# Rows of x first on ScalarE, an exponential ahead of copies, constants loaded later

## The chip, the core and the metric

The kernel runs on one core of a Trainium2 chip. Five engines work side by side, each on its own queue in program order: TensorE (PE) multiplies, VectorE (DVE), ScalarE (ACT) and GpSimd (POOL) work on elements, SyncE (SP) issues loads. 16 transfer engines move data. TensorE writes to PSUM, in eight banks, from which VectorE or ScalarE copy into SBUF. The metric is the time of one execution on the device in microseconds. Before the change three runs gave 613.08, 617.48 and 619.69, median 617.48.

## What is computed

Attention of 8 batches and 8 heads on 576 positions with 64 dimensions: the first four heads look at the last 32 positions, the other four at every 32nd one. Its result, as 4608 rows x of 512, goes through a mixture of 8 experts: each row to the one expert of the largest gate logit.

```python
scores = np.where(masks[None, :, :, :], scale * np.matmul(q, k.transpose(0, 1, 3, 2)), -1000000000.0)
attn = np.exp(scores - np.max(scores, axis=-1, keepdims=True))
attn = attn / (np.sum(attn, axis=-1, keepdims=True) + 1e-09)
x = np.matmul(attn, v)            # then as rows: [4608, 512]
logits = x @ w_gate               # [4608, 8]
expert_idx = np.argmax(logits, axis=1)
for e in range(E):
    mask = expert_idx == e
    h = np.maximum(x[mask] @ w1[e], 0.0)
    out[mask] = gate_w[mask, None] * (h @ w2[e])
```

## The kernel before

**Attention.** Each batch has five tasks (`BANK_PAIRS`), each one PSUM bank of scores: tasks 0 and 1 the local heads, 2 to 4 the rest and the strided heads. A task is worked in a pipeline over the loop index `i` (the loop at lines 977 to 1023, where the order of TensorE is as written):
- `stage_s`: a matmul that writes the mask into the bank (line 480), score matmuls on it (491 for tasks 0 and 1, 499 and 505 for the others), then `softmax`: largest value (407) and subtraction (411) on VectorE, the exponential (412) on ScalarE, sum (414) and reciprocal (416) on VectorE, the product with the reciprocal (421) on GpSimd.
- `stage_t`, three tasks later: four transposes of the probabilities on TensorE (542), copied from PSUM by ScalarE (`evac`, line 169), into `pTl` with two copies for tasks 0 and 1, into `pT` with one for the others.
- `av_local`, `av_strided`, four tasks later: the products with v (567, 556), copied by ScalarE into `xT`.

Tasks 3 and 4 are scored together, so four sets of scores of batch 0 come ahead of the first copies. `load_qk` and `load_v` issue the loads of q, k and v on SyncE's queue up to five tasks ahead, when the buffer is free; those of the first batch come one behind the other.

**Rows and routing.** Two batches make a group of 1152 rows. `logits` multiplies `xT` with the gate weights (616), and finds the gate; `xrows` transposes 128 rows back on TensorE (608), copies them from PSUM on ScalarE into `xr`, behind which GpSimd has written the gate in 16 columns (605), and stores them from ScalarE's queue (611). There are 36 such row tiles. They and the logits share two banks of PSUM (`XTAGS`: y for the first two groups, v for the others), so a copy that is late holds up whatever takes the bank next. `route` computes each row's place in its expert's list (matmuls 675, 677, 658), `slot_tables` the tables for the rows beyond the base lists.

**Experts.** From about 118 us on, the expert windows on the first three groups (`fillers`) run between the attention tasks; after the attention come the rest of them, then the base windows of all experts. Weights are loaded in 1 MB pieces (228), split into two parts by ScalarE (238) and VectorE (239), and used by three matmuls each (331 to 333, 320 to 322).

**Start.** ScalarE's queue first issues three loads: mask and identity (960), gate weights `wg` (390), and `cst` (391), the constants of the routing: a triangle, the numbers 0 to 127 and others. `load_more` also converts them: the triangle on VectorE (393), the numbers on GpSimd (398, 399).

**Order.** On engines other than TensorE a scheduler sets the order, by a priority that falls with the place in the program; `tc.high_priority(offset=n)` lifts instructions by n places. `issue_after(a, b)` puts a behind b on their queue without a wait.

Of the kernel before, what the change touches and what calls it, by code (L numbers as in the profile page):

```python
# [13 lines left out]
ALU = mybir.AluOpType  # L14
# [6 lines left out]
E, DM, DF = 8, 512, 1024  # L21
# [9 lines left out]
GT = GB * S // 128  # L31
# [27 lines left out]
X_ENG = "aa"  # L59
# [91 lines left out]
def moe_attn(ctx, tc, qk, vv, wg, wcat, blob0, blob, out):  # L151
    nc = tc.nc
# [10 lines left out]
    def evac(which, out, in_):  # L163
        if which == "v":
            nc.vector.tensor_copy(out=out, in_=in_)
        elif which == "g":
            nc.gpsimd.tensor_copy(out=out, in_=in_)
        else:
            copied[0] = nc.scalar.copy(out=out, in_=in_)

    copied = [None]
# [5 lines left out]
    cst = const.tile([128, blob.shape[1]], F32, name="cst")  # L177
    tri_f = cst[:, 0:128]
    iota_sb = cst[:, 128:256]
    wexp_sb = cst[:, 256:256 + E]  # L180
    tokhi_sb = cst[:, 256 + E:256 + E + NT]
# [51 lines left out]
    after = []  # L233
# [35 lines left out]
    def issue_after(ins, prev):  # L269
        tc.add_manual_dep(ins.ins, prev.ins.name,  # L270
                          mybir.DependencyInfo(mybir.DependencyClass.NoSync, mybir.DependencyReason.SCHED_ONLY),
                          reason="order on the engine's queue")
# [84 lines left out]
    with ExitStack() as actx:  # L357
# [29 lines left out]
                                      in_=lmask_f[:, 64 * m:64 * m + 64].unsqueeze(1).broadcast_to([128, x1 - x0, 64]))  # L387

        def load_more():
            nc.scalar.dma_start(out=wg_sb.rearrange("p c e -> p (c e)"), in_=wg)  # L390
            nc.scalar.dma_start(out=cst, in_=blob)
            nc.vector.memset(ones_b, 1.0)
            nc.vector.tensor_copy(out=tri_b, in_=tri_f)
            for t in (pfall, tokp, keyp, keysp):
                nc.gpsimd.memset(t, 0.0)
            for t in ex_tiles:
                nc.gpsimd.memset(t[:, :, E:], EPS)
            nc.gpsimd.tensor_copy(out=tokp[:, :, 0:GT], in_=tokhi_sb.rearrange("p (g t) -> p g t", t=GT))
            nc.gpsimd.tensor_copy(out=iota2, in_=iota_sb.unsqueeze(2).broadcast_to([128, 128, 2]))
            zrow = xrp.tile([128, XW], F32, name="xr")[0:1]  # L400
            nc.gpsimd.memset(zrow, 0.0)
            nc.gpsimd.dma_start(out=xd[0:1, :], in_=zrow)

        def softmax(sb):
            sv = sb.rearrange("p (n k) -> p n k", k=64)[:, :, 0:USED]
            nm = small.tile([128, 8], F32, name="nm")
            largest = nc.vector.tensor_reduce(out=nm, in_=sv, axis=AX.X, op=ALU.max)
            prob = next_prob()
            whole = prob.rearrange("p (n k) -> p n k", k=64)
            pv = whole[:, :, 0:USED]  # L410
            shifted = nc.vector.tensor_tensor(out=pv, in0=sv, in1=nm.unsqueeze(2).broadcast_to([128, 8, USED]), op=ALU.subtract)
            exps.append(nc.scalar.activation(out=pv, in_=pv, func=AF.Exp, scale=0.125))
            sm = small.tile([128, 8], F32, name="sm")
            total = nc.vector.tensor_reduce(out=sm, in_=whole, axis=AX.X, op=ALU.add)
            ri = small.tile([128, 8], F32, name="ri")
            begun.append((largest, shifted, total, nc.vector.reciprocal(out=ri, in_=sm)))  # L416
            if len(begun) == 3:
                issue_after(begun[1][0], begun[0][2])
                issue_after(begun[2][0], begun[0][3])
                issue_after(begun[1][2], begun[2][1])  # L420
            product[0] = nc.gpsimd.tensor_tensor(out=pv, in0=pv, in1=ri.unsqueeze(2).broadcast_to([128, 8, USED]), op=ALU.mult)  # L421
            return prob

        loaded = {}
        exps = []
        begun = []

        def in_order(d, b):
            if b == 0:
# [20 lines left out]
        def load_qk(i):  # L450
            if i < len(tasks):
                b, k = tasks[i]
                x = halves(qk, b, QKO, k)
                if k < 2:
                    for h in range(2):
                        in_order(nc.sync.dma_start(out=two(qkl[k][h:128:2, h * LK:h * LK + LQ + LK]),
                                                   in_=x[h:128:2]), b)
                    return
                t = inp.tile([128, max(QKW[2:])], F32, name="qk")
                loaded[b, "qk", k] = t  # L460
                in_order(nc.sync.dma_start(out=two(t[:, 0:QKW[k]]), in_=x), b)
# [68 lines left out]
        def stage_s(b, *ks):  # L530
            sb = [bank("s") for _ in ks]
            gens = [scores(b, k, s) for k, s in zip(ks, sb)]
            for _ in zip_longest(*gens):
                pass
            return [softmax(s) for s in sb]
# [3 lines left out]
        def stage_t(b, k, prob):  # L539
            tb = bank("t")  # L540
            for x in range(4):
                nc.tensor.transpose(tb[:, x * 128:(x + 1) * 128], prob[:, x * 128:(x + 1) * 128], ident)
            if k < 2:
                evac("a", pTl[k][0:64, 0, :], tb[0:64, :])
                evac("a", pTl[k][64:128, 1, :], tb[64:128, :])
                return
            pT = pts.tile([128, 512], F32, name="pT")
            evac("a", pT, tb)
            pTs[b, k] = pT
# [53 lines left out]
        def xrows(g, c, xT):  # L603
            xr = xrp.tile([128, XW], F32, name="xr")
            nc.gpsimd.tensor_copy(out=xr[:, DM:XW], in_=gates[g][:, c:c + 1].broadcast_to([128, XW - DM]))
            xb = bank(XTAGS[g])
            for pr in range(4):
                nc.tensor.transpose(xb[:, pr * 128:(pr + 1) * 128], xT[:, pr, c * 128:(c + 1) * 128], ident)
            evac(X_ENG[c % 2], xr[:, 0:DM], xb)
            T = g * GT + c  # L610
            nc.scalar.dma_start(out=xd[1 + T * 128:1 + (T + 1) * 128, :], in_=xr)

# [165 lines left out]
        def slot_tables():  # L778
# [1 line left out]
            nc.vector.scalar_tensor_tensor(out=rem, in0=tiles_sb, scalar=-128.0, in1=cnt, op0=ALU.mult, op1=ALU.add)  # L780
            nc.vector.tensor_scalar(out=rem, in0=rem, scalar1=0.0, scalar2=None, op0=ALU.max)
            it128 = rt.tile([128, 32], F32, name="it128")
            nc.vector.tensor_scalar(out=it128, in0=iota_sb[:, 0:32], scalar1=128.0, scalar2=None, op0=ALU.mult)
            cmp = scratch(E * 32).rearrange("p (e k) -> p e k", k=32)
            nc.vector.tensor_tensor(out=cmp, in0=rem.unsqueeze(2).broadcast_to([128, E, 32]),
                                    in1=it128.unsqueeze(1).broadcast_to([128, E, 32]), op=ALU.is_gt)
# [189 lines left out]
        with tc.manual_schedule(engines={mybir.EngineType.PE}):  # L976
            for i in range(nt + LAG_AV):
                it = i - LAG_T
                if 0 <= it < nt:
                    stage_t(*tasks[it], pvs.pop(it))  # L980
                step()
                ia = i - LAG_AV
                if 0 <= ia < nt:
                    b, k = tasks[ia]
                    g, bb = divmod(b, GB)
                    if g not in xTs:
                        xTs[g] = xtp.tile([128, 4, GB * S], F32, name="xT")
                        Ls[g] = rt.tile([128, GT, E], F32, name="L", bufs=2)
                        dls[g] = rt.tile([128, GT, E], F32, name="dl", bufs=2)
                        gates[g] = rt.tile([128, GT], F32, name="gt", bufs=2)  # L990
                    step()
                exps.clear()
                if i < nt:
                    filling()
                    b, k = tasks[i]
                    if k == PAIR[0]:
                        pvs[i], pvs[i + 1] = stage_s(b, *PAIR)
                    elif k not in PAIR:
                        pvs[i], = stage_s(b, k)
                    load_qk(i + NBK)  # L1000
                if 0 <= ia < nt:
                    b, k = tasks[ia]
                    if k == 0:
                        queue.extend(late)
                        late.clear()
                    elif k == 1:
                        av_local(b, xTs[g], bb * S)
                    elif k == 3:
                        av_strided(b, 0, xTs[g], bb * S)
                        for e in exps:  # L1010
                            issue_after(e, copied[0])
                    elif k == 4:
                        av_strided(b, 1, xTs[g], bb * S)
                        for e in exps:
                            issue_after(e, copied[0])
                        (late if b < EG * GB - 1 else queue).extend(row_steps(g, bb, xTs[g], Ls[g]))
                        if b == B - 1:
                            filling()
                if 0 <= ia:
                    load_v(ia + NV - 1)  # L1020
                step()
                filling()
                step()
# [348 lines left out]
```

## Time and profile before

| | |
|---|---|
| median of three runs | 617.48 us |
| the profiled execution | 617.55 us |
| its span | 615.8 us |
| TensorE busy | 588.2 us, 96% |
| VectorE, ScalarE, GpSimd busy | 349.9, 284.2, 153.9 us |
| moved by the transfer engines | 133.04 MB, 216 GB/s in the mean |

TensorE is the busiest engine by far. Its idle time lies in the first 215 us and at the very end; a stretch of the profile tells which engine it waited for there. The granted clock is the one at which TensorE's array runs, 1.00 for 2.4 GHz and 0.50 for 1.2 GHz. An idle time stands in brackets at the instruction that ended it, with what released it.

### The profile page before, as it was taken

How to read it: one execution, taken by the hardware profiler on the slowest of the kernel's cores; microseconds unless marked ns; L12 is line 12 of the kernel's file. 1: busy time of each engine (PE TensorE's matmuls, PEld its weight loads, DVE VectorE, ACT ScalarE, POOL GpSimd, SP SyncE). 2: the span in 40 equal slices, each digit the busy share in tenths (PEclk: the TensorE clock that was granted, in tenths of full speed). 3: DMA queues.
4: the chain of work that ended last, by engine and by line, in shares of the span. 5: the costliest groups of instructions: out<-in, count | busy, mean ns of one | idle time of the engine just before them, and what ended most of it. 6: DMA issues, size and time to landing. Idle time of an engine off the chain costs nothing. (4 is left out here: it accounts for less than half of the span.)

```text
span 615.8 us, 14290 instructions
## 1 busy us (share of the span) xinstructions
PE 588.2 (96%) x5930; PEld 489.5 (80%) x5930; DVE 349.9 (57%) x684; ACT 284.2 (46%) x508; POOL 153.9 (25%) x202
## 2 busy tenths in 40 slices
PE   5899989989899999999999999999999999999996
PEld 3677766768788788888888998788988879987885
DVE  6779878868653699975534445234443335452342
ACT  2566757755755555645333434324333324442241
POOL 4333332431220331060630332014402003020031
PEclk9899999999999999999999999999999999999999
DMA  8989989997557666595862565355644537254101
GB/s 293 306 290 337 333 265 341 364 357 257 184 177 286 211 235 226 184 347 195 297 230 81 191 208 177 122 212 195 217 171 172 205 132 288 79 177 147 60 38 53
DMA packets 43203, 133.04 MB, mean 216 GB/s; under 512 B 4602, under 2 KB 17280, under 8 KB 34944
## 3 DMA queue, kind: packets, MB, share of 16 engines
q1 hardware_dynamic: 29504, 89.14, 42.3%
q10 hardware_dynamic: 7344, 22.71, 10.1%
q0 software_dynamic: 6288, 20.26, 9.0%
q8 instruction: 47, 0.77, 0.5%
q14 instruction: 20, 0.16, 0.1%
HBM read 112.91 MB, written 19.63 MB: 215 GB/s over the span
## 5 line engine op out<-in xcount | busy, mean ns | idle before, releaser
L239 DVE TENSOR_TENSOR wlo<-raw,whi 128x1024 fp32r<-128x1024 f32 x104 | 126.0, 1231 | 71.6 <-ACT whi L238 65.2
L331 PE MATMUL t<-xh,whi 128*128 128x256 f32 (+2 forms) x384 | 133.9, 349 | 0.8 <-ACT whi L238 0.8
L238 ACT CAST whi<-raw 128x1024 fp32r<-128x1024 f32 x104 | 106.1, 1050 | 58.6 <-PE s L322 43.8
L333 PE MATMUL t<-xh,wlo 128*128 128x256 f32 (+2 forms) x384 | 130.0, 339 | 0.9 <-DVE wlo L239 0.8
L332 PE MATMUL t<-xl,whi 128*128 128x256 f32 (+2 forms) x384 | 129.8, 338 | 0.0
L338 DVE SCALAR_TENSOR_TENSOR hl<-t,hh 128x256 fp32r<-128x256 f32 (+2 forms) x96 | 53.1, 554 | 121.6 <-ACT hh L337 121.2
L337 ACT ACTIVATE hh<-t 128x256 fp32r<-128x256 f32 (+2 forms) x96 | 47.2, 492 | 141.7 <-PE t L333 134.9
L331 PEld LDWEIGHTS t<-xh,whi 128*128 128x128 f32 x384 | 72.6, 189 | 10.6 <-issue 3.2
L333 PEld LDWEIGHTS t<-xh,wlo 128*128 128x128 f32 x384 | 72.7, 189 | 7.2 <-DVE wlo L239 1.9
L332 PEld LDWEIGHTS t<-xl,whi 128*128 128x128 f32 x384 | 72.7, 189 | 5.8
L320 PE MATMUL y<-whi,hh 128*128 128x512 f32 x192 | 76.2, 398 | 0.0
L321 PE MATMUL y<-wlo,hh 128*128 128x512 f32 x192 | 75.7, 394 | 0.0
L322 PE MATMUL y<-whi,hl 128*128 128x512 f32 x192 | 75.4, 394 | 0.0
L421 POOL TENSOR_TENSOR prob<-prob,ri 128x504 f32<-128x504 f32 x40 | 41.0, 1031 | 92.0 <-DVE ri L416 61.9
L287 POOL DMA_INDIRECT out_dram<-y,oids x28 | 31.7, 1131 | 102.1 <-DVE y L286 96.1
L259 POOL DMA_INDIRECT xg<-xd,ids x28 | 35.7, 1275 | 59.7 <-PE v L306 39.4
L322 PEld LDWEIGHTS y<-whi,hl 128*128 128x128 f32 x192 | 36.0, 188 | 7.7 <-DVE hl L338 0.2
L320 PEld LDWEIGHTS y<-whi,hh 128*128 128x128 f32 x192 | 36.0, 188 | 5.9
L321 PEld LDWEIGHTS y<-wlo,hh 128*128 128x128 f32 x192 | 36.1, 188 | 5.5
L321 PE MATMUL s<-wlo,hh 128*128 128x512 f32 x96 | 37.8, 393 | 0.0
L322 PE MATMUL s<-whi,hl 128*128 128x512 f32 x96 | 37.5, 391 | 0.0
L320 PE MATMUL s<-whi,hh 128*128 128x512 f32 x96 | 37.5, 391 | 0.0
(233 smaller groups left out, 829.7 us busy)
## 6 DMA issues: line engine op xcount, KB each, us to landing
raw<-in_wcat_dram SPq DMA_DIRECT2D x52, 1024.0 KB
sraw<-in_wcat_dram ACTq DMA_DIRECT2D x12, 1024.0 KB
xd<-xr ACTq DMA_DIRECT2D x36, 264.0 KB
qkl<-in_qk_dram SPq DMA_DIRECT2D x32, 264.0 KB
vl<-in_vv_dram SPq DMA_DIRECT2D x16, 512.0 KB
vt<-in_vv_dram SPq DMA_DIRECT2D x16, 256.0 KB
qk<-in_qk_dram SPq DMA_DIRECT2D x8, 484.0 KB
qk<-in_qk_dram SPq DMA_DIRECT2D x8, 432.0 KB
```

The costliest lines, as they stand in the source:

```text
L238: j = nc.scalar.copy(out=hi[:, sl], in_=raw[:, sl])
L239: i = nc.vector.tensor_tensor(out=lo[:, sl], in0=raw[:, sl], in1=hi[:, sl].bitcast(F32), op=ALU.subtract)
L259: lastp[0] = nc.gpsimd.indirect_dma_start(out=xg, out_offset=None, in_=xd[0:rows, :], in_offset=bass.IndirectOffsetOnAxis(ap=idc, axis=0))
L320: nc.tensor.matmul(yb[t], hh[:, ts], whi[:, w], start=(j == 0), stop=False)
L321: nc.tensor.matmul(yb[t], hh[:, ts], wlo[:, w], start=False, stop=False)
L322: nc.tensor.matmul(yb[t], hl[:, ts], whi[:, w], start=False, stop=(j == 7))
L331: nc.tensor.matmul(hb[:, 0:n], whi[:, w], xh[:, dc, :], start=(dc == 0), stop=False)
L332: nc.tensor.matmul(hb[:, 0:n], whi[:, w], xl[:, dc, :], start=False, stop=False)
L333: nc.tensor.matmul(hb[:, 0:n], wlo[:, w], xh[:, dc, :], start=False, stop=(dc == 3))
L337: nc.scalar.activation(out=hh[:, 0:n], in_=hb[:, 0:n], func=AF.Relu)
L338: nc.vector.scalar_tensor_tensor(out=hl[:, 0:n], in0=hb[:, 0:n], scalar=0.0, in1=hh[:, 0:n].bitcast(F32), op0=ALU.max, op1=ALU.subtract)
L421: product[0] = nc.gpsimd.tensor_tensor(out=pv, in0=pv, in1=ri.unsqueeze(2).broadcast_to([128, 8, USED]), op=ALU.mult)
```

## The change

- The loads of `wg` and `cst` are issued behind the first exponential on ScalarE (`load_constants`, called in the first pass of the loop). Their conversions are placed behind the fifth task's subtraction (VectorE) and product (GpSimd) (`convert_constants`).
- The first copy out of the first transposes is placed behind the third exponential.
- The copy of the row tiles has a priority of 60 places more.
- One table of the slot tables (`it128`) is placed behind the row lists (`after[0]`).

```diff
         def load_more():
-            nc.scalar.dma_start(out=wg_sb.rearrange("p c e -> p (c e)"), in_=wg)
-            nc.scalar.dma_start(out=cst, in_=blob)
             nc.vector.memset(ones_b, 1.0)
-            nc.vector.tensor_copy(out=tri_b, in_=tri_f)
 ...
-            nc.gpsimd.tensor_copy(out=tokp[:, :, 0:GT], in_=tokhi_sb.rearrange("p (g t) -> p g t", t=GT))
-            nc.gpsimd.tensor_copy(out=iota2, in_=iota_sb.unsqueeze(2).broadcast_to([128, 128, 2]))
 ...
+        def load_constants():
+            for d in (nc.scalar.dma_start(out=wg_sb.rearrange("p c e -> p (c e)"), in_=wg),
+                      nc.scalar.dma_start(out=cst, in_=blob)):
+                issue_after(d, all_exps[0])
+
+        def convert_constants():
+            issue_after(nc.vector.tensor_copy(out=tri_b, in_=tri_f), begun[4][1])
+            for d in (nc.gpsimd.tensor_copy(out=tokp[:, :, 0:GT], in_=tokhi_sb.rearrange("p (g t) -> p g t", t=GT)),
+                      nc.gpsimd.tensor_copy(out=iota2, in_=iota_sb.unsqueeze(2).broadcast_to([128, 128, 2]))):
+                issue_after(d, product[0])
 ...
             exps.append(nc.scalar.activation(out=pv, in_=pv, func=AF.Exp, scale=0.125))
+            all_exps.append(exps[-1])
 ...
                 evac("a", pTl[k][0:64, 0, :], tb[0:64, :])
+                if (b, k) == tasks[0]:
+                    issue_after(copied[0], all_exps[2])
                 evac("a", pTl[k][64:128, 1, :], tb[64:128, :])
 ...
-            evac(X_ENG[c % 2], xr[:, 0:DM], xb)
+            with tc.high_priority(offset=60):
+                evac(X_ENG[c % 2], xr[:, 0:DM], xb)
 ...
-            nc.vector.tensor_scalar(out=it128, in0=iota_sb[:, 0:32], scalar1=128.0, scalar2=None, op0=ALU.mult)
+            issue_after(nc.vector.tensor_scalar(out=it128, in0=iota_sb[:, 0:32], scalar1=128.0, scalar2=None, op0=ALU.mult), after[0])
 ...
+                    if i == 0:
+                        load_constants()
+                    elif i == 4:
+                        convert_constants()
```

ScalarE from its first instruction on, before (`prob` with a number is a task's probabilities, `pTl` their transposes, `t` and `v` PSUM banks):

```order
L960 DMA cst_70<-in_blob_dram 128x320
L390 DMA wg_sb<-in_wg_dram 128x128
L391 DMA cst<-in_blob_dram 128x311
L412 ACT_TABLE_LOAD
L412 ACTIVATE prob_134<-prob_134 128x8x63
L412 ACTIVATE prob_135<-prob_135 128x8x63
L169 COPY pTl_148<-t 64x512 x2
L412 ACTIVATE prob_136<-prob_136 128x8x63
L169 COPY pTl_149<-t 64x512 x2
```

and with the change:

```order
L971 DMA cst_70<-in_blob_dram 128x320
L418 ACT_TABLE_LOAD
L418 ACTIVATE prob_134<-prob_134 128x8x63
L400 DMA wg_sb<-in_wg_dram 128x128
L401 DMA cst<-in_blob_dram 128x311
L418 ACTIVATE prob_135<-prob_135 128x8x63
L418 ACTIVATE prob_136<-prob_136 128x8x63
L169 COPY pTl_148<-t 64x512 x2
L169 COPY pTl_149<-t 64x512 x2
```

The two loads moved behind the first exponential, and the third exponential ahead of the first two copies.

ScalarE at the last task pair of batch 3 (66 to 69 us of the profile before), before (`xT` is the attention's result, `xr` a row tile):

```order
L169 COPY xT<-v 128x18x15
L169 COPY xT<-v 128x18x2
L169 COPY xT<-v 128x18x15
L169 COPY xT<-v 128x18x2
L412 ACTIVATE prob_137<-prob_137 128x8x63
L169 COPY xr<-y 128x512
L412 ACTIVATE prob_133<-prob_133 128x8x63
L611 DMA xd<-xr 128x528
L169 COPY pTl_149<-t 64x512 x2
```

and with the change:

```order
L169 COPY xT<-v 128x18x15
L169 COPY xT<-v 128x18x2
L169 COPY xT<-v 128x18x15
L169 COPY xr<-y 128x512
L169 COPY xT<-v 128x18x2
L418 ACTIVATE prob_137<-prob_137 128x8x63
L418 ACTIVATE prob_133<-prob_133 128x8x63
L622 DMA xd<-xr 128x528
L169 COPY pTl_149<-t 64x512 x2
```

The row copy moved from between the two exponentials to ahead of both. Over the whole program seven of the 36 row copies move from behind a softmax exponential to ahead of it, and no row copy moves the other way; the store of the rows moves back in several places.

ScalarE in the rows of the last batch (205 to 211 us), before (`whi` is half of a weight piece, `hh` the hidden layer, `ex` the gate's exponential):

```order
L284 ACTIVATE y<-y,xg 128x512
L634 ACTIVATE ex_139<-dl 128x3x8
L169 COPY xr<-v 128x512
L634 ACTIVATE ex_138<-dl 128x3x8
L238 CAST whi<-raw 128x1024
L611 DMA xd<-xr 128x528
L337 ACTIVATE hh<-t 128x256
L169 COPY xr<-v 128x512 x2
```

and with the change:

```order
L284 ACTIVATE y<-y,xg 128x512
L169 COPY xr<-v 128x512
L645 ACTIVATE ex_139<-dl 128x3x8
L645 ACTIVATE ex_138<-dl 128x3x8
L238 CAST whi<-raw 128x1024 x2
L169 COPY xr<-v 128x512 x2
L337 ACTIVATE hh<-t 128x256
L622 DMA xd<-xr 128x528
```

Two row copies moved from behind the store and `hh` to ahead of them, and the second half of a weight cast moved in ahead of the two copies.

On TensorE the order is the same up to the rows of the last batches; from there transposes of rows, expert matmuls and the matmuls of the routing interleave differently in some places.

## Rows read from the trace of the kernel before

**Rows 1.** Busy by stretch: us; busy of PE, PEld, DVE, ACT, POOL; PEclk, DMA share, GB/s.

```profile
258.00:608.00 350.00, 349.98 (x2066) 297.08 (x2065) 155.14 (x204) 133.10 (x202) 79.60 (x88) 1.00 0.50 177
```

**Rows 2.** Waits of TensorE, whole span: total, times, longest.

```profile
PE t L542 <- issue: 1.5, 1, 1.5
...
PE y L675 <- ACT xr L169: 0.5, 1, 0.5
```

**Rows 3.** Timeline of TensorE, 5 to 24 us: start, us, what [idle before <-releaser].

```profile
5.46 0.58 PE L480 MATMUL s<-mask_b,identb 128*128 128x512 bf16 x1 [5.46 <-DVE mask_b L386]
6.62 1.94 PE L491 MATMUL s<-qkl 128*32 128x128 f32 x32 [0.57 <-DMA qkl<-in_qk_dram]
...
18.03 1.12 PE L542 MATMUL t<-cst,prob 128*128 128x128 f32 x4 [1.32 <-POOL prob L421]
...
19.50 1.94 PE L491 MATMUL s<-qkl 128*32 128x128 f32 x32
```

**Rows 4.** Busy by stretch, columns as in rows 1.

```profile
5.00:10.00 5.00, 3.97 (x54) 2.53 (x57) 2.13 (x6) 0.00 (x0) 1.57 (x4) 1.00 1.01 345
...
18.00:21.50 3.50, 3.47 (x39) 2.38 (x41) 2.29 (x4) 1.62 (x3) 0.00 (x0) 0.51 1.06 381
```

**Rows 5.** Timeline, 0 to 13 us, columns as in rows 3.

```profile
1.17 0.45 ACTq L390 DMA_DIRECT2D wg_sb<-in_wg_dram  x1
...
5.75 0.23 DVE L393 CAST tri_b<-cst 128x128 bf16<-128x128 f32 x1 [0.34 <-DMA cst<-in_blob_dram]
...
6.02 0.40 POOL L399 CAST iota<-cst 128x256 bf16<-128x256 f32 x1
...
12.73 0.62 ACT L412 ACTIVATE prob<-prob 128x504 f32<-128x504 f32 x1 [2.06 <-DVE prob L411]
```

**Rows 6.** Timeline of ACT, DVE and POOL, 12 to 18 us.

```profile
13.32 0.68 DVE L411 TENSOR_TENSOR prob<-s,nm 128x504 f32<-128x504 f32 x1
...
14.01 1.19 ACT L169 COPY pTl<-t 64x512 f32<-64x512 f32 x2 [0.66 <-PE t L542]
...
14.63 0.20 DVE L416 RECIPROCAL ri<-sm 128x8 f32<-128x8 f32 x1
...
14.97 1.03 POOL L421 TENSOR_TENSOR prob<-prob,ri 128x504 f32<-128x504 f32 x1 [1.71 <-DVE ri L416]
...
15.22 0.62 ACT L412 ACTIVATE prob<-prob 128x504 f32<-128x504 f32 x1
...
15.88 0.69 DVE L414 TENSOR_REDUCE sm<-prob 128x8 f32<-128x512 f32 x1 [1.05 <-ACT prob L412]
...
16.95 1.03 POOL L421 TENSOR_TENSOR prob<-prob,ri 128x504 f32<-128x504 f32 x1 [0.94 <-DVE ri L416]
```

**Rows 7.** Timeline of SyncE's issues, 9 to 13 us.

```profile
9.10 3.62 SPq L456 DMA_DIRECT2D qkl<-in_qk_dram  x4
```

**Rows 8.** Timeline of ACT and PE, 65 to 70 us.

```profile
65.34 0.86 ACT L169 COPY xT<-v 128x270 f32<-128x270 f32 x4 [0.44 <-PE y L608]
...
66.45 0.50 PE L658 MATMUL y<-bb,am 128*128 128x80 bf16 x9
66.78 0.62 ACT L412 ACTIVATE prob<-prob 128x504 f32<-128x504 f32 x1 [0.59 <-DVE prob L411]
...
67.31 0.57 ACT L169 COPY xr<-y 128x512 f32<-128x512 f32 x1
...
67.93 1.66 PE L616 MATMUL y<-xT,wg_sb 128*32 128x384 f32 x8 [0.99 <-ACT xr L169]
```

**Rows 9.** Timeline of ACT and PE, 206 to 211 us.

```profile
206.45 1.05 ACT L238 CAST whi<-raw 128x1024 fp32r<-128x1024 f32 x1
...
208.84 0.33 ACTq L611 DMA_DIRECT2D xd<-xr  x1
...
209.49 1.07 ACT L169 COPY xr<-v 128x512 f32<-128x512 f32 x2
...
210.12 0.66 PE L608 MATMUL v<-cst,xT 128*128 128x128 f32 x4 [1.09 <-ACT xr L169]
```

More of the change, by code (lines that the diff above doesn't have):

```diff
@@ L426, in moe_attn @@
         begun = []
+        all_exps = []
         def in_order(d, b):
```

## The prediction

> **What bounds the kernel now.** The median of the three runs is 617.48 us; the profiled execution took 617.55, of which 615.8 is the span, so the sum below is made against 617.55, which stands 0.07 above the median. I read the busy time by stretches first. From 258 to 608 us TensorE is busy 349.98 of 350 us at the full clock [rows 1]: the end is set by TensorE's work, and whatever makes TensorE reach this stretch earlier moves the end by as much, unless a load is late. So the next view is the list of what TensorE waited for, and then the timeline around each wait that the diff can touch: the first 20 us [rows 3 to 7], where TensorE starts late and waits for the softmax chain, and two places where it waits for a copy of rows of x out of PSUM [rows 8, 9]. The list holds a third wait on such a copy, 0.5, and one of 1.5 that no engine ended ("issue") [rows 2]. I take the second for no part of the change; it tells how far a stall of that sort can move the time by itself.
>
> **Constants behind the first exponential.** The two loads carry 128x128 and 128x311 floats, 64 and 155.5 KB, together 219.5 KB or 0.225 MB. They leave the start and come back after 10 us. In the start TensorE's mask matmul runs from 5.46 to 6.04, and the first score matmul waits 0.57 more, to 6.62, for q and k [rows 3]. At the 345 GB/s of 5 to 10 us [rows 4] the removed bytes take 0.65, more than the wait, but a part of them has run before q and k begin to move; ends 0 and 0.57, I take **0.5**, near the upper end, because the transfer engines are full there (share 1.01 [rows 4]).
> On ScalarE's queue one issue takes 0.45 [rows 5], two 0.9; they now stand between the first and the second exponential, where ScalarE idles 2.06 [rows 5], so they cost nothing; without that cover the second exponential would be 0.9 later. VectorE's cast of the triangle, 0.23, waited 0.34 for its load, and GpSimd's longer cast took 0.40 [rows 5]. Both go behind the fifth softmax's subtraction and product. VectorE waits for exponentials before the sums there (as it does 1.05 in [rows 6]). Would the constants be in? The first exponential ended at 10.67 (12.73 less the idle 2.06), so they are issued by 11.6; in the start the same load, issued at 1.62 behind the gate weights, was in at 5.75, 4.1 later [rows 5]. That makes 15.7, ahead of the fifth subtraction, which follows the third sum by two maxima and two subtractions. Cost 0. The table of multiples of 128 moves behind the last row lists, off the routing chain; TensorE runs expert work there, which covers it, so nothing again.
> The Trainium skill ("DMA: Bandwidth & Descriptors", section "Issuing engines are not separate DMA queues") speaks against the move: transfers issued from different engines run on the same 16 engines and interleave, so ScalarE's bytes stay in the way of q and k loads, only at another time. By that rule the start gains and the next loads lose the same, which is case C below; the trace agrees so far that the share is still 1.06 from 18 to 21.5 [rows 4].
>
> **Third exponential ahead of the first copies.** Its subtraction ends at 14.00; before, two copies (14.01, 1.19) stand ahead of it and it runs at 15.22 [rows 6]. Now it can run at 14.01 to 14.63. Its sum then starts when VectorE is free, at 14.83 instead of 15.88; sum 0.69 and reciprocal 0.20 end at 15.7; GpSimd has the product before it until 16.00 [rows 6], so that one starts at 16.00 instead of 16.95, and TensorE's third transposes at 17.08 instead of 18.03 [rows 3]: 0.95 earlier. The two copies become 0.62 later; the product that reads them stands on TensorE behind the next scores (19.50 and 1.94 [rows 3]), so nobody waits.
> What is late next is the load of the second batch's first q and k, issued from 9.10 to 12.7 [rows 7], behind all that was issued earlier and with the transfer engines full. The scores on it begin at 19.50 [rows 3]. When it landed no row says: by the 4.1 us of the constants [rows 5] at 16.8, at the latest at 19.50. With more issued in front of it than the constants had, I put it near the latest, at 19.0; the constants, now moved in between, keep it from getting earlier. So of 0.5 + 0.95 only **0.5** is left at these scores; ends 0 and 1.52.
>
> **Rows of x first.** The copies get a higher rank on ScalarE. The order shows seven of the 36 passing from behind a softmax exponential to ahead of it; the transposes on TensorE keep their order up to the routing of the last batches.
> At 67 us the copy (67.31) stands behind an exponential that waits for VectorE until 66.78; TensorE's gate product then waits 0.99 for the PSUM bank [rows 8]. Now the copy stands among the four copies that begin at 65.34 and take 0.86; with 0.57 for itself all are done by 66.8. TensorE's work before ends at 66.95, so the gate product starts there instead of 67.93: **0.98**; ends 0 and 0.99.
> At 94 us (0.5 [rows 2]) the copy keeps its neighbours in the order: 0.
> At 209 us ScalarE's queue stands at a store of rows (208.84) until GpSimd has written the gate column, and two row copies behind it hold TensorE for 1.09 [rows 9]. Now the second half of a weight cast (1.05, its data there, as the first half ran at 206.45) and then both copies stand ahead of that store: cast to 208.55, first copy to 209.1, where TensorE is ready at 209.03. That gives 1.0; the hidden layer's activation, at 209.21 ahead of the copies, now comes behind them at 209.6, and its product on TensorE may wait for that. I take **0.7**; ends 0 and 1.09.
>
> **The sum:** 617.55 - 0.5 - 0.98 - 0.7 = 615.4.
>
> **The rivals.**
> A. TensorE's clock stays up. After the wait of 1.32 before the third transposes [rows 3] the granted clock is 0.51 from 18 to 21.5 [rows 4], the lower level, 1.2 GHz; the score matmuls take 1.94 there for 32 [rows 3]. If the shorter wait keeps it at the upper level, these 1.94 halve, some 0.9 less: 614.5. Against it: the wait that goes here comes back in part as one for the load. The Trainium skill ("TensorE: Matmul & The Clock Gate", Part 1) says that the array's clock is held down by default and that activity lets it go; by that the fall goes with the idle time, and the trace agrees that it came right behind it.
> B. The copies go ahead, and the exponentials pay: slower. The place is each of the seven; the price one copy's step on ScalarE, 1.07 - 0.57 = 0.50 [rows 8, 9], when the exponential is ready and TensorE's next transposes wait for its product. If all seven count and the gains at 67 and 209 are lost: 617.55 - 0.5 + 3.5 = 620.5. It decides from the point where softmax has no slack before its transposes. For it: such waits stand in the first 20 us. Against it: at 67 us the exponential waited for VectorE, not for ScalarE.
> C. Nothing reaches the end: the 219.5 KB, put back ahead of the second batch's load, make that load 0.65 later and so take all of the start (with the engines full [rows 4], it lands no earlier than now), and the freed waits on copies are taken over by the next thing TensorE needs: 617.5. For it: the loads that are late next in the start; against it: the two waits on copies lie 50 and 190 us behind, where [rows 8, 9] name nothing else that is late.
>
> **How the numbers follow.** Forecast 0.47, A 0.20, B 0.12, C 0.21. The forecast is the likeliest, 615.4. Low end: all upper ends, 0.57 + 0.95 + 0.99 + 1.09 = 3.6, with A's 0.9 and one stall of 1.5 [rows 2] not met again: 617.55 - 6.0 = 611.6. High end: C with such a stall more, 619.0; B's full price is left out. A measurement of this kernel can tell about 1% from no change, 6.2 us, so faster means below 611.3 and slower above 623.7: all cases lie within but for the outermost. Faster 0.13, within 0.83, slower 0.04.
>
> **What would show it.** In the changed profile: first scores at about 6.1; third transposes at 16.6 or sooner; the second batch's scores at about 19, waiting for a load and not for a product; no wait on a row copy above 0.3 near 66 and 208; the stretch of full TensorE work some 2 us earlier, as full as now. Wrong it would be if the second batch's scores start well before 18.5 (the load was not the limit), if the granted clock stays up after 18, or if waits on exponentials or casts appear in TensorE's list that are not in the one of before.

## The result: slower by half a per cent

The changed kernel takes 618.35 us (median of 22 runs), the kernel before 615.68 in the same measurement: ratio 1.0052, 95% interval 1.0032 to 1.0072, some 3 us slower. The forecast was 615.4, a gain of 2. The profiled execution took 617.78, span 616.0, so its steps are read against [rows 1 to 9], whose execution took 617.55. A profile shows one execution of a kernel.

The bound is as before: from 258 to 608 us TensorE is as full as in [rows 1]. The columns are those of [rows 1]; the first two lines are to be read against [rows 4].

```profile
5.00:10.00 5.00, 4.54 (x66) 2.88 (x65) 1.77 (x4) 0.59 (x1) 1.01 (x2) 1.00 0.89 277
18.00:21.50 3.50, 1.72 (x56) 1.55 (x58) 2.21 (x6) 1.20 (x3) 1.25 (x2) 1.00 0.78 257
258.00:608.00 350.00, 349.98 (x2067) 297.18 (x2065) 155.59 (x204) 133.70 (x203) 79.45 (x88) 1.00 0.49 177
```

So what counts is how early TensorE gets there. Its list of waits (total, times, longest) shows two that were not there or were small before, on `bb` and on `qkl`, and between them a longer one at the scores that no engine or load ended ("issue"):

```profile
PE v L669 <- DVE bb L665: 3.2, 1, 3.2
PE s L513 <- issue: 2.5, 4, 1.2
PE s L499 <- DMA qkl<-in_qk_dram: 2.0, 1, 2.0
```

**The start.** TensorE's timeline, to be read against [rows 3]:

```profile
5.97 1.94 PE L499 MATMUL s<-qkl 128*32 128x128 f32 x32
...
16.66 0.66 PE L550 MATMUL t<-cst,prob 128*128 128x128 f32 x4 [0.33 <-POOL prob L428]
...
19.78 1.08 PE L499 MATMUL s<-qkl 128*32 128x128 f32 x32 [2.02 <-DMA qkl<-in_qk_dram]
...
31.10 0.42 PE L513 MATMUL s<-qk 64*54 64x54 f32 x16 [1.18 <-issue]
...
32.82 1.23 PE L627 MATMUL y<-xT,wg_sb 128*32 128x384 f32 x8
```

The first scores come 0.65 earlier, the third transposes 1.37, the clock stays at 1.00 from 18 to 21.5, and still the second batch's scores come 0.28 later, behind a wait of 2.02 for their load. The first gate product, 32.47 before, is 0.35 late. SyncE's four issues of the second batch's first loads, to be read against [rows 7], are late too, and these are SyncE's waits around them:

```profile
12.03 6.15 SPq L464 DMA_DIRECT2D qkl<-in_qk_dram  x4
```

```profile
SPq L476 <- DMA qk<-in_qk_dram: 1.9, 1, 1.9
SPq L464 <- DMA cst<-in_blob_dram: 1.9, 1, 1.9
SPq L464 <- DMA wg_sb<-in_wg_dram: 1.4, 1, 1.4
SPq L464 <- DMA vl<-in_vv_dram: 0.9, 1, 0.9
```

The order of the two queues says why: each load takes one of eight counters in turn, and must wait until the counter's last user has landed. Here the constants have the two (DMAHW0, DMAHW1) that the third and fourth of the four loads get next, so SyncE stands until the constants have landed:

```
ACT  L400 DMA wg_sb<-in_wg_dram 128x128 [waits DMAHW0_49]
ACT  L401 DMA cst<-in_blob_dram 128x311 [waits DMAHW1_49]
SP   L464 DMA qkl_147<-in_qk_dram 64x2x528 [waits DMAHW0_49,PE_49]
SP   L464 DMA qkl_147<-in_qk_dram 64x2x528 [waits DMAHW1_49]
```

The first two of the four, which the scores at 19.78 read, have other counters (DMAHW6, DMAHW7). They go out at 12.03 and 13.01 instead of 9.10 and 9.75 because, without the constants at the start, each counter comes round two loads sooner: the load of v ahead of them (L476) waits 1.9 for one of q and k, and the first of them 0.9 for one of v. By 22 us 6.19 MB have moved, 7.00 before.

That the late issue is what delays the scores at 19.78 is not shown, and other runs speak against it. In e15 (below), with the constants at the start and the issues from 9.54 on, the scores start at 19.78 as well:

```profile
9.54 4.20 SPq L458 DMA_DIRECT2D qkl<-in_qk_dram  x4
```

```profile
19.78 1.08 PE L493 MATMUL s<-qkl 128*32 128x128 f32 x32 [1.67 <-DMA qkl<-in_qk_dram]
```

The second of the two loads lands, by the last step of its counter in the trace, at 19.65 in the change and in e15, and at 18.89 in the kernel before. Over all profiles it lands between 18.41 and 19.65, in the mean at 19.1 in the seven with the constants behind the first exponential and at 19.0 in the seven with them at the start. After these scores, up to the first gate product, the longest wait of the change is the 1.18 at 31.10 (0.46 before), which no engine or load ended; in other profiles it lies between none (e3) and 2.56 (e1).

**67 us**, to be read against [rows 8]: the wait on the row copy is gone, but the gate product now stops in its middle, for 0.88 that no engine ended:

```profile
67.38 0.84 PE L627 MATMUL y<-xT,wg_sb 128*32 128x384 f32 x4
69.09 0.84 PE L627 MATMUL y<-xT,wg_sb 128*32 128x384 f32 x4 [0.88 <-issue]
```

**The last rows**, to be read against [rows 9]. TensorE (first and last row), ScalarE and VectorE:

```profile
205.94 0.66 PE L618 MATMUL v<-cst,xT 128*128 128x128 f32 x4
...
206.94 0.34 ACTq L622 DMA_DIRECT2D xd<-xr  x1
...
208.90 0.59 ACT L169 COPY xr<-v 128x512 f32<-128x512 f32 x1 [0.66 <-PE v L618]
...
214.18 0.59 ACT L169 COPY xr<-v 128x512 f32<-128x512 f32 x1 [4.69 <-DMA xd<-xr]
...
215.17 0.39 ACT L337 ACTIVATE hh<-t 128x256 fp32r<-128x256 f32 x1 [0.40 <-ACT xr L169]
...
215.59 0.42 DVE L338 SCALAR_TENSOR_TENSOR hl<-t,hh 128x256 fp32r<-128x256 f32 x1 [3.01 <-ACT hh L337]
215.93 0.36 DVE L661 TENSOR_TENSOR bm<-iota,keyp 128x400 bf16<-128x400 bf16 x1
...
217.07 0.78 PE L669 MATMUL v<-bb,am 128*128 128x80 bf16 x9 [3.17 <-DVE bb L665]
```

The wait of 1.09 at 210 is gone, and TensorE reaches these transposes 4.18 ahead of before (205.94 against 210.12; 3 of it was already there at 200). Then the last row copy finds all five row buffers taken; its own is free only when the store issued at 206.94 has landed, at 214.18. ScalarE stands 4.69, the hidden layer's activation `hh` behind it is late, `hl` on VectorE waits for `hh`, the routing's tables `bm` and `bb` stand behind `hl`, and TensorE, whose order has the routing's products next, stands 3.17.

In the kernel before, the last copy stands ahead of the same `hh` and its buffer is freed by the same store, but the store is not waited for:

```profile
213.97 0.59 ACT L169 COPY xr<-v 128x512 f32<-128x512 f32 x1 [0.51 <-PE v L677]
215.13 0.39 ACT L337 ACTIVATE hh<-t 128x256 fp32r<-128x256 f32 x1 [0.57 <-PE t L333]
```

There the store goes out at 208.84 [rows 9], 1.28 ahead of the transposes at 210.12, and has landed by 212.55, 3.7 later. In the change it stands behind two row copies and an `hh`, goes out 1.00 behind those transposes, and lands 7.2 later. Beside it goes a load of 1 MB of weights, which in the kernel before goes out only at 219.71: the second half of the weight cast, now ahead of the copies, is followed by VectorE's half, and that frees the load's buffer:

```profile
206.88 0.33 SPq L228 DMA_DIRECT2D raw<-in_wcat_dram  x1
```

In the six profiles with this load right ahead of the store (the change, e2, e4, e13, e14, e15) the store takes 6.7 to 7.3 us, in the other eleven 3.6 to 4.0. No run has the store's new place without the load, so that the load slows the store is argued, not shown.

Right behind this the clock falls to half:

```profile
209.00:213.90 4.90, 4.90 (x43) 4.40 (x41) 2.35 (x12) 0.49 (x1) 0.00 (x0) 1.00 0.88 346
213.90:217.07 3.17, 0.00 (x1) 0.00 (x1) 1.43 (x5) 1.84 (x3) 0.19 (x1) 0.84 0.66 252
217.07:222.90 5.83, 5.83 (x26) 5.15 (x27) 3.33 (x9) 1.40 (x3) 1.96 (x2) 0.50 0.30 77
```

At 308 us the same matmul runs at 308.68, before at 308.44: the lead of 4.18 has become a lag of 0.24. This place cost 4.4 in this execution. It costs some 4 in each profile in which the copy waits ahead of `hh`: from the third-last row transposes (205.94 here) to one expert product (the 100th-last on line 322, 336.33 here) TensorE needs 128.8 to 130.4 us in the change, e2 and e4, and 124.6 to 126.4 in the other fourteen profiles, the kernel before among them (126.0).

### The profile page after: what moved, and what is told of

Same layout as the page of the kernel before. It is cut to its first block, busy times and chain, and to the rows that moved or that the text cites. A ratio compares the mean times of both kernels' runs of the same rounds, so it can differ in the third digit from the quotient of the medians.

```text
span 616.0 us, 14278 instructions
## 1 busy us (share of the span) xinstructions
PE 584.9 (95%) x5916; PEld 489.0 (79%) x5930; DVE 350.7 (57%) x684; ACT 283.7 (46%) x508; POOL 153.0 (25%) x202
## 5 line engine op out<-in xcount | busy, mean ns | idle before, releaser
L338 DVE SCALAR_TENSOR_TENSOR hl<-t,hh 128x256 fp32r<-128x256 f32 (+2 forms) x96 | 53.3, 555 | 124.6 <-ACT hh L337 122.6
L259 POOL DMA_INDIRECT xg<-xd,ids x28 | 33.9, 1211 | 56.1 <-PE v L306 39.4
```

Source lines behind the costliest of these rows:

```text
L259: lastp[0] = nc.gpsimd.indirect_dma_start(out=xg, out_offset=None, in_=xd[0:rows, :], in_offset=bass.IndirectOffsetOnAxis(ap=idc, axis=0))
L338: nc.vector.scalar_tensor_tensor(out=hl[:, 0:n], in0=hb[:, 0:n], scalar=0.0, in1=hh[:, 0:n].bitcast(F32), op0=ALU.max, op1=ALU.subtract)
```

## Experiments

All are timed in five rounds against the kernel before on the same chip. Executions of one kernel spread over some 7 us (610.77 to 617.68 for the kernel before in the last series), so a ratio is known to 0.2 to 0.35%. The profiles tell where time goes, each in one execution. The theories that the expectations name by number are stated in those of e1 (1 to 3), e5 (4) and e13 (5).

**e1**, the row copies' priority undone.

```diff
-            with tc.high_priority(offset=60):
-                evac(X_ENG[c % 2], xr[:, 0:DM], xb)
+            evac(X_ENG[c % 2], xr[:, 0:DM], xb)
```

> The change without the higher priority of the row copies: loads behind the first exponential, third exponential ahead of the copies and the moved table stay. Theory 1 (the loss lies at the last routing: a row copy that waits for the store of an earlier row tile stands ahead of a hidden layer's activation, VectorE's tables come late, TensorE waits 3.2 us for them and then runs 3.4 us at half clock, together about 5 us): that wait is gone, the time is 613 to 615.7 against 615.7 before. Theory 2 (the loss lies in the start: the second batch's first loads are issued only when the moved constants have landed): nothing changes, about 618.3, 0.4% above before. Theory 3 (row copies ahead of exponentials delay the softmax in many places): about 615.5.

1.0041 [1.0018, 1.0063]. The wait for `bb` is gone, and the loss mostly stays: theory 1 is not enough. This edit undoes the gains of the copies as well.

**e2**, the priority alone, on the kernel before (the diff of e1 the other way).

> The kernel before with the higher priority of the row copies alone. Theory 1: the wait of about 3 us for the routing's tables near 214 us is there, the time 617.5 to 619.5 against 615.7 before. Theory 2: no loss, 614.5 to 615.7, and no such wait. Theory 3: 617.5 to 619.5, with waits on exponentials spread over 30 to 210 us.

1.0016 [0.9990, 1.0041]. ScalarE stands 4.78 at the same copy, `hh` starts at 215.39, TensorE waits for it and the clock falls. That is the place of theory 1, though the wait is for `hh` and not for the tables; yet the time is hardly above before, below the 617.5 to 619.5 that the theory forecast.

```profile
214.40 0.59 ACT L169 COPY xr<-v 128x512 f32<-128x512 f32 x1 [4.78 <-DMA xd<-xr]
...
215.82 0.50 PE L320 MATMUL y<-whi,hh 128*128 128x512 f32 x1 [1.79 <-ACT hh L337]
```

**e3**, the change without the priority in the last group (`offset=60 if g < NG - 1 else 0`).

> The change, but the row copies of the last group of batches keep their old priority. Theory 1: no wait for the tables near 214 us, 612.5 to 615, below before. Theory 2: about 618.3, as with the whole change. Theory 3 (most of the copies that pass an exponential lie in the earlier groups): about 617.5.

1.0027 [0.9999, 1.0055]. No wait and full clock at 214 to 222, but no gain, against the forecast of theory 1; the interval only just holds 1. So I looked for a further cost in the start or the table.

**e4**, the constants behind the seventh exponential.

```diff
-                issue_after(d, all_exps[0])
+                issue_after(d, all_exps[6])
...
-                    if i == 0:
+                    if i == 6:
                         load_constants()
-                    elif i == 4:
+                    elif i == 8:
                         convert_constants()
```

The conversions follow two tasks later.

> The whole change, but the two loads of constants are issued behind the seventh exponential instead of the first, and converted two tasks after that. Theory 1: the wait near 214 us stays and so does the loss: 617 to 618.5; the wait of 2.0 us for the second batch's load near 19 us shrinks below 1. Theory 2: 615 to 616, the loss is gone. Theory 3: 617.5 to 618.5.

1.0053 [1.0025, 1.0082]. SyncE's second-batch loads go out from 9.74 again, the first gate product starts at 31.56, and the wait for `bb` (2.8) and the fall of the clock are there. Theory 2 alone falls as well; theory 4 (both) was formed here. The counters bind here too, only later: after 25 us SyncE stands 3.2 until the gate weights have landed. No wait of TensorE up to the first gate product names a load there.

**e5**, the priority in the first three groups alone, on the kernel before (as in e3).

> The kernel before with the higher priority of the row copies in the first three groups alone. Theory 4 (two causes: the row copies of the last group cost about 3 us near 214, those of the earlier groups give about 1.5 back; and in the start the loads that the moved constants hold up cost about 2): 613 to 614.5 against 615.1 before. Theory 1 (only the last group costs): 613 to 614.5 as well. Theory 3 (row copies delay exponentials everywhere): 616 to 618.

0.9982 [0.9960, 1.0004]; theory 3 falls. Against e2 the last group costs 1.0016 / 0.9982 = 1.0034, 2.1 us, by intervals of 0.0026 and 0.0022.

**e6**, the constants alone (`load_constants`, `convert_constants`), on the kernel before.

> The kernel before with the constants loaded behind the first exponential and converted later, alone. Theory 4: SyncE's loads of the second batch wait for the landing of the constants and are issued 3 to 5 us later than before, some 0.5 MB less are moved by 22 us, and TensorE waits for loads of q and k between 18 and 32 us; 616.5 to 617.5 against 615.1. Theory 1: 614.5 to 615.2, the start gains its 0.6. If the third exponential is what costs, about 615.

1.0047 [1.0023, 1.0071], but its profile shows another reason than expected. Without the change's fourth edit the scheduler pulls the table `it128` up on VectorE, ahead of the third subtraction, where it waits for the constants; TensorE waits 3.92 behind it:

```profile
16.66 0.18 DVE L791 TENSOR_SCALAR it<-cst 128x32 f32<-128x32 f32 x1 [3.96 <-DMA cst<-in_blob_dram]
...
17.48 0.61 PE L488 MATMUL s<-mask_b,identb 128*128 128x512 bf16 x1 [3.92 <-DVE prob L417]
```

**e7**, the third exponential alone (`issue_after(copied[0], all_exps[2])`).

> The kernel before with the third exponential ahead of the first copies, alone. Theory 4: the third transposes come 0.9 earlier, the second batch's first load lands as before, 614.3 to 615.2 against 615.1. If the exponential is what costs in the start (the first copies late, with them a PSUM bank and a load), 616.5 to 617.5.

0.9984 [0.9961, 1.0008]. The second batch's scores start at 19.23, and the first gate product at 31.53, 0.94 earlier than in the kernel before. The time is at the edge of its interval: no gain is shown.

**e8**, the table alone (`issue_after(..., after[0])`).

> The kernel before with the one table placed behind the row lists, alone. Theory 4: 614.8 to 615.5, no change. If the moved table is what costs (the tables of the rows beyond the base lists come late, or the order around the last routing moves), 616.5 to 617.5, with a wait of TensorE between 215 and 300 us.

0.9996 [0.9971, 1.0021]: no change.

**e9**, constants and table, and **e10**, the same with the loads issued from GpSimd.

```diff
-            for d in (nc.scalar.dma_start(out=wg_sb..., in_=wg),
-                      nc.scalar.dma_start(out=cst, in_=blob)):
-                issue_after(d, all_exps[0])
+            for d in (nc.gpsimd.dma_start(out=wg_sb..., in_=wg),
+                      nc.gpsimd.dma_start(out=cst, in_=blob)):
+                issue_after(d, product[0])
```

> The kernel before with the constants loaded behind the first exponential and the table placed behind the row lists, without the third exponential's move and without the row copies' priority. Theory 4: SyncE's loads of the second batch are issued 3 us later than before, because each load takes one of a few counters in turn and waits until its earlier user has landed, here the constants; 0.5 MB less by 22 us, TensorE some 1 to 2 us later by 36 us than before; 616 to 617.5 against 615. Rival (the loss of the constants alone came only from the table's wait on VectorE): 614.4 to 615.2, 0.6 faster from the start on.

> As the run before, but the two loads are issued from GpSimd behind the first product, where they use other counters than SyncE's loads. Theory 4: SyncE's loads go out as before (the second batch's from about 9 us), at least 6.9 MB by 22 us, TensorE at 36 us 0.3 to 0.8 earlier than in the kernel before; later stages have another order on several engines, so the time is read only by that stage. Rival (the bytes themselves are in the way, wherever they are issued): 6.2 to 6.5 MB by 22 us and TensorE late by 1 to 2 us at 36.

e9: 1.0011 [0.9981, 1.0041]; e10: 1.0030 [1.0003, 1.0057], its order differing later. e9 misses what theory 4 forecast for it, 616 to 617.5: SyncE's loads go out 2.5 us later than before and 6.47 MB are moved by 22 us, as expected, but the first gate product starts at 32.12, 0.35 earlier than in the kernel before. SyncE, and TensorE's second-batch scores, in e9:

```profile
11.60 5.59 SPq L464 DMA_DIRECT2D qkl<-in_qk_dram  x4
...
18.80 1.08 PE L499 MATMUL s<-qkl 128*32 128x128 f32 x32 [0.46 <-DMA qkl<-in_qk_dram]
```

and in e10:

```profile
8.15 4.30 SPq L464 DMA_DIRECT2D qkl<-in_qk_dram  x4
...
18.88 1.08 PE L499 MATMUL s<-qkl 128*32 128x128 f32 x32 [0.54 <-DMA qkl<-in_qk_dram]
```

From GpSimd the constants (issued at 12.58 and 13.19, some 3 us later than in e9, so two things differ) hold up no issue of SyncE: no wait names them, and 6.92 MB are moved by 22 us instead of 6.47. But the second batch's scores do not come earlier for it: the loads that go out 3.45 ahead land at the same time, the second of them at 18.75 against 18.67. The first gate product starts at 31.53 instead of 32.12; the wait without a releaser at the scores ahead of it differs by more than that (0.73 against 1.66). e10's later stages I did not trace, so its time stays unexplained.

**e11**, the third exponential with e5's priority; **e12**, the whole change with both losses mended (e4's and e3's edits).

> The kernel before with the third exponential ahead of the copies and the row copies' priority in the first three groups: the two parts that looked like gains. Theory 4: their gains add, 612.5 to 613.5 against 615. If each was noise: 614.5 to 615.3.

> The whole change with both losses mended: constants issued behind the seventh exponential, and no priority for the row copies of the last group. Theory 4: 612.3 to 613.5 against 615, no loss near 19 or 214 us. If the moved constants cost something that does not depend on their place: 615 to 616.5.

e11: 1.0008 [0.9975, 1.0042]; e12: 1.0022 [0.9992, 1.0051]. Both miss: the gains seen in profiles do not add up to a shorter time. For e12 the expectation had the other case too, moved constants that cost wherever they stand, and that is the nearer one.

**e13**, the change without the priority of the very last copy (`offset=60 if g < NG - 1 or c < 8 else 0`), and **e14**, the change with a sixth row buffer.

```diff
-        xrp = tctx.enter_context(tc.tile_pool(name="xrp", bufs=5))
+        xrp = tctx.enter_context(tc.tile_pool(name="xrp", bufs=6))
...
-            ls = rt.tile([128, 384], F32, name="ls", bufs=2)
+            ls = rt.tile([128, 384], F32, name="ls", bufs=1)
```

> The whole change, but the very last of the 36 row copies keeps its old priority: on ScalarE it then stands behind the hidden layer's activation instead of ahead of it. Theory 5 (this one copy, which waits for the store that frees its buffer, holds the activation, VectorE and TensorE): no wait for the tables near 214 us above 0.5, TensorE between 209 and 262 us 3 to 4 us faster than in the changed kernel and full clock there; 616 to 617 against 615.1 before. If the priority of the other row copies of the last group costs it: the wait of about 3 us stays, 617.5 to 619.

> The whole change with six buffers for row tiles instead of five (one buffer of the logits' copy taken for it, so the logits may wait a little): the order around the last copies is the same but for one store, but the last copy's buffer was stored from 20 us earlier. Theory 5: the copy does not wait, ScalarE runs the activation at about 211 instead of 215, no wait for the tables above 0.5, and no half clock near 216. If the order of the queues alone makes the loss: the wait of about 3 us stays.

e13: 1.0014 [0.9985, 1.0043], e14: 1.0022 [0.9995, 1.0050]. In e13 `hh` runs ahead of the copy, which still waits for the store, but TensorE does not stop for anything behind it:

```profile
210.97 0.38 ACT L337 ACTIVATE hh<-t 128x256 fp32r<-128x256 f32 x1 [1.64 <-DVE ri L699]
...
213.92 0.59 ACT L169 COPY xr<-v 128x512 f32<-128x512 f32 x1 [2.56 <-DMA xd<-xr]
```

In e14 the last two copies run at 211.59 in one go. Neither has a wait for `bb` in its list, and TensorE's clock is full, as here in e14:

```profile
214.00:218.00 4.00, 3.95 (x32) 3.35 (x31) 3.32 (x12) 2.57 (x4) 0.00 (x0) 1.00 0.99 370
218.00:222.00 4.00, 4.00 (x28) 3.65 (x27) 3.81 (x11) 0.93 (x2) 0.67 (x1) 1.00 0.53 163
```

That settles the place: one copy, ahead of `hh`, whose buffer a late store holds. With that copy behind `hh` (e13, e15), with one more buffer (e14), or with the store early as in the kernel before (the other eleven), the granted clock is 1.00 from 214 to 222; in the change, e2 and e4 it falls, to 0.50, 0.78 and 0.68 from 218 to 222.

**e15**, third exponential and e13's priority, constants at the start.

> The kernel before with the third exponential's move and the priority for all row copies but the very last, constants at the start as before. Theory 5: keeps what each part gave (about 1 in the start, 1 at 209), 612.5 to 614 against 615.1. If the parts give nothing that can be measured: 614.7 to 615.5.

0.9991 [0.9966, 1.0015]; the gains that theory 5 adds up miss again. No version beats the kernel before by more than the measurement is uncertain.

## Why the prediction was wrong

**The base** held: the end moves with TensorE's arrival at 258.

**Rows at 209 us: "I take 0.7"; this step failed.** The gain itself came: the change's lead over the kernel before goes from 3.0 at 200 us to 4.18 at these transposes. But I put the weight cast's second half and both copies ahead of the store at 208.84 and gave the store's delay no price. I asked what the first two copies wait for, not what the last one needs: a buffer out of five, held by that store. And I said that the product behind the activation "may wait", without following its queue to VectorE, the tables and TensorE. The runs show in place of a gain of 0.7 a wait of 4.69 on ScalarE and of 3.17 on TensorE, with the lower clock behind it: 4.4 in the change's profile, gone in e13 and e14, and 1.8 us in the fit below. That the routing's products moved ahead in TensorE's order I noted, and gave it no price.

**Constants: "they cost nothing".** The 0.65 at the first scores came (0.5 forecast): they start at 5.97 or 5.98 in all ten profiles with the constants moved, at 6.43 to 7.19 in the seven with them at the start. The issues did hide in ScalarE's idle time. The constants took 7.8 us to land (9.81 to 17.57) where I took 4.1 from the start; TensorE did not wait for them.

"So of 0.5 + 0.95 only 0.5 is left at these scores" was right in its limit, the load, put at 19.0 (18.89 in the kernel before, 19.0 to 19.1 in the means), and too large in what is left: the scores start at 19.32 in the mean of the five profiles with both moves and the constants behind the first exponential (the change, e1, e3, e13, e14), at 19.45 in that of the four with neither (before, e2, e5, e8), 0.13 earlier. What I did not look for, though the order of the queues shows it, is that the moved constants change when SyncE may issue; what that costs is not shown, as these loads land no later for it.

The first gate product starts at 32.30 to 32.85 in those four, at 31.10 to 31.53 with the third exponential alone or with row copies (e7, e11, e15), and at 32.01 to 33.70 with that and the constants behind the first exponential (those five). The means of the last two, 31.35 and 33.03, lie 1.7 apart, of which 0.13 is there at the second batch's scores; the rest comes in waits without a releaser and, in e3, e13 and e14, at a lower clock. As the constants without the exponential (e9, 32.12) cost nothing there, 1.7 is not the price of the constants alone. So in time they cost (1.8 us in the fit), and where stays open.

The Trainium skill ("DMA: Bandwidth & Descriptors", section "Issuing engines are not separate DMA queues") says that DMAs run on the same 16 DMA engines and interleave, whichever engine started them. e10 against e9 agrees for the landing (18.75 and 18.67); what the issuing engine changed there is only when SyncE could issue (8.15 and 11.60), by the counters.

**The table: "nothing again"** was right for the edit (e8), wrong as a reason: it is what keeps the moved constants from stopping VectorE (e6).

**Third exponential.** 0.95 forecast at the transposes: they start 11.41 behind the first scores in the profiles without the move (e6 apart) and 10.43 to 10.88 with it, so 0.53 to 0.98 came. In e7, alone, the first gate product comes 0.94 earlier. Why its time gains no more than 0.0016, I can't say.

**Rows at 67 us: "0.98".** The wait on the copy went, and 0.88 came back in the next product; what ends that wait stays open. It is not shown to come from the copy: e1, e7 and e9, with the copy's old rank, have it too (0.17, 1.11, 0.46).

**Rivals.** B had the sign: copies ahead delay ScalarE's other work. Its place and price were wrong, not a softmax exponential at 0.50 a copy but one activation, at 4.4 in the change's profile. C has the load 0.65 later; in the change's profile it is 0.76 later (19.65 against 18.89), but over the profiles no later. A's clock did stay up at 18 us in the change, and the time did not follow; in e3 and e14, with the same start, it fell (0.58 and 0.55 from 18 to 21.5).

**The sum as measured.** A least-squares fit of 14 of the ratios (without e6 and e10; e4 and e12 taken as the same constants), weighted by their intervals and made as if the parts add, gives in us of 615: constants with table +1.8 ± 0.5, third exponential +0.2 ± 0.5, row copies without the last -0.7 ± 0.4, the last row copy +1.8 ± 0.6; together 3.1, the change's 3.2. That the last copy costs 4.4 in the change's profile and 1.8 in the fit is not explained. Where the constants' 1.8 is lost no profile shows: at the third-last row transposes the profiles with early copies and the constants behind the first exponential (the change, e3, e13, e14) stand at 205.8 to 208.6, those with early copies and the constants at the start (e2, e5, e11, e15) at 206.1 to 207.4. In e4 and e12 the first gate product starts at 31.56 and 32.29, in e7, e11 and e15 at 31.35 in the mean: the later place mends most of the start, but their times do not show it; that stays open too.

## What to carry to other kernels

Before lifting an instruction on an in-order engine, list everything it waits for, its output buffer's last store included; look what the same lift does to that store, which may move back and meet a load that now goes out earlier; and then follow what stands behind the instruction through the next engines until TensorE. Judge by the last instruction of the moved sort, not the first. Before moving a load, look which completion counters it shares: in the order of the queues, every later load on another queue that waits for the same counter now waits for this one's landing. But do not take a later issue for a later landing: here loads issued 3 us apart landed together.

## What the runs showed of the hardware

A store of one row tile (264 KB), issued at 206.94 right behind a load of 1 MB, freed its buffer only 7.2 us later (346 GB/s were moved from 209 to 213.9); with the same five buffers e13 shows 206.78 to 213.92. In the kernel before, without such a load beside it, it took 3.7 (208.84 to 212.55). The second batch's first loads landed at 18.67 and 18.75 when issued at 12.59 (e9) and 9.04 (e10). A TensorE pause of 3.17 us at 214 was followed by 5.83 us at the lower clock level, and one of 1.79 in e2 by a granted clock of 0.78 from 218 to 222. At 19 us a pause of 2.02 (the change) left it at 1.00, while pauses of 1.66 (e3) and 1.59 (e14) at the same place were followed by score matmuls that take 1.94 for 32 instead of 1.08.
